# Three transposes per 128 slots in place of two, and a different order at the start of a conv-and-experts kernel

## The chip, the cores and the metric

The kernel runs on one core of one Trainium2 chip. The metric is the device time of that core in microseconds (us), less is better. Times of the kernel before are the median of three runs; a profiled execution stands beside them.

## What is computed

Two stages, in float32, over 8 sequences of 3584 tokens with 192 channels each. The first is a causal convolution along the sequence, with 7 taps per head (8 heads of 24 channels), the taps normalised by a softmax. The second sends each token through one of 8 experts:

```python
logits = x @ w_gate                       # 8 per token
local  = sigmoid(x @ w_local)
for each token s of a sequence, in order:
    fresh = argmax(logits[s])
    e = fresh if s == 0 or local[s] < 0.5 else prev_e
    prev_e = e
    h = maximum(x[s] @ w1[e], 0)          # 192 -> 1024
    out[s] = softmax(logits[s])[e] * (h @ w2[e])   # 1024 -> 192
```

A token may thus take the expert of the token before it, so the choice is a scan along the sequence.

## The kernel before

**Parts, slots and blocks.** The 28672 tokens are cut into 16 parts of 1792 (`PT`). A part is convolved, its experts are chosen (routing), and each of its rows, with its weight, number and channels, is scattered to a slot of its expert in DRAM (`slots`, one indirect DMA per 128 or 112 rows, issued by POOL in `put`, L777). A block is one or two units of 128 slots of one expert. The first 35 blocks have one unit each, then come 87 blocks of two units and 20 of one (142 in all, 229 units of 128 slots). Which expert a block belongs to is worked out on the chip (`first_table`, `table`) and read by SP from `tabi` when it loads the block's rows (L913) and weights (L906). A block may load its rows once the scatters of its group of parts are done. Four buffers hold weights, six hold rows.

**A block.** `hidden` multiplies the rows, turned so that channels lie on partitions, with the first weights (L963); ScalarE applies the relu and writes `hT` (L968). `turn` then transposes the rows of the next block on TensorE (L360) and ScalarE copies the result out of PSUM to `xT`. `output` multiplies `hT` with the second weights into two PSUM tiles `yps` (L980), one per half of the contraction; ScalarE scales one (L988), VectorE adds the other (L992), and POOL sends the rows to `out` (L996). There are two `yps` buffers in all, so a block's two tiles are those that the block before used. TensorE works on two halves of 64 rows at a time, and a row of 192 channels is three groups of 64 (`KD`, `DR`). A row in DRAM holds its 192 channels and a repeat of 64 of them.

In `turn`, the kernel before transposes channels 0 to 127 and then channels 128 to 191 with their repeat. Each half of the rows goes to all 128 partitions, so the second transpose gives the third group on both halves of the partitions, and the three groups are brought into place by three ScalarE copies: L947 on 128 partitions, and L949 twice on 64.

**The convolution.** The first two parts are convolved on TensorE (`wide`), the others on VectorE: ScalarE writes the first tap of a head (L378), VectorE adds the six others (L388), 48 such operations per part. `conv` is a generator; `step(time)` takes operations from it, or from a part's routing, until their estimated times add up to `time`. `step` stands between the pieces of a block. The order in which instructions are written is the order in which each engine runs them.

**The start.** `wide_route` is the routing of the first two parts in pieces that end at a `yield`: (1) and (2) the best logit, the exponent and `fc`; (3) the transposes to `rps` on TensorE; (4) the scan to `run`, its transpose `bps`, and the norm; (5) `oh` and its sums on TensorE; (6) slots (`upto`, `pos`), after which 16 scatters are ready to be put; (7) the tables. The first two blocks don't read their rows from DRAM: VectorE builds 0/1 matrices (`hots`, L550), TensorE gathers the rows with them (`gather`, L556), and ScalarE copies them out (`gathered`, L561 to L563). The kernel before interleaves the gathers with the whole of `route1`, the second part's routing, and issues the 16 scatters of the first part in groups of 5, 3, 2, 2 and 4, all but the first group each after a named instruction of `route1` (`puts_behind`). Then the blocks begin.

Of the kernel before, what the change touches and what calls it, by code (L numbers as in the profile page):

```python
# [17 lines left out]
P = 128  # L18
# [63 lines left out]
def kernel(  # L82
# [100 lines left out]
        nc.vector.tensor_copy(c.rearrange("p h k -> p (h k)"), cps[:, H:H + H * KC])  # L183
    wgb, wgq = wg[:, :3, :], wg[:, 3:, :]

    got, mark = {}, {}

# [7 lines left out]
    def wide(g, xv, y_sb, both):  # L195

        lps = yps_p.tile([P, 512], F32, name="yps")[:, :4 * TB].rearrange("p (q s) -> p q s", s=TB)  # L200
        count = [0]

        def mine():
            count[0] += 1
            return both and count[0] % 2 == 0

        def convolve(half, heads):
            bs = slice(half * NH, (half + 1) * NH)
            for h in heads:
                ps = hps_p.tile([P, 512], F32, name="hps")[:TB, :NH * GS]  # L210
                nc.tensor.matmul(ps, lhsT=hank[:NI, h, :],
                                 rhs=xv[:NI, bs, h * GS:(h + 1) * GS], start=True, stop=True)
                to = y_sb[:TB, bs, Y0 + h * GS:Y0 + (h + 1) * GS]
                at = ps.rearrange("p (b d) -> p b d", d=GS)
                if mine():
                    nc.vector.tensor_scalar(to, at, rz[:TB, h:h + 1], None, Alu.mult)
                else:
                    nc.scalar.activation(to, at, Act.Copy, scale=rz[:TB, h:h + 1])
                yield

        def again(half):
            bs = slice(half * NH, (half + 1) * NH)
            nc.gpsimd.tensor_copy(yr[:, bs, :], y_sb[:TB, bs, Y0 + P:Y0 + D])
            nc.gpsimd.tensor_copy(y_sb[:TB, bs, Y0 + D:IX], y_sb[:TB, bs, Y0 + P:Y0 + D])

        def turned(half, qs):
            at = half * 3 * NH // 2
            for q in qs:
                tps = hps_p.tile([P, 512], F32, name="hps")[:, :4 * TB].rearrange(
                    "p (u s) -> p u s", s=TB)  # L230
                for u in range(4):
                    b = half * NH + (q * 4 + u if q < 2 else 2 * u)
                    src = (y_sb[:TB, b, Y0:Y0 + P] if q < 2
                           else yr[:, b:b + 2, :].rearrange("p b d -> p (b d)"))
                    nc.tensor.transpose(tps[:, u, :], src, identity=ident[:TB, :TB])
                leave = nc.vector.tensor_copy if mine() else nc.scalar.copy
# [26 lines left out]
        products()  # L263
        if both:
            nc.vector.tensor_copy(lsb[:, :2, :], lps[:, :2, :])
            nc.scalar.copy(lsb[:, 2:, :], lps[:, 2:, :])
        else:
            nc.scalar.copy(lsb, lps)
        yield
        ltp = yps_p.tile([P, 512], F32, name="yps")[:TB].rearrange("p (q c) -> p q c", c=P)  # L270
        for q in range(4):
            nc.tensor.transpose(ltp[:, q, :], lsb[:, q, :], identity=ident)
        lt = sm.tile([P, NB, E + 1], F32, name="lt")[:TB]
        mark["lt", g] = nc.vector.tensor_copy(lt.rearrange("p (j q) e -> p j q e", q=4),
                              ltp.rearrange("p q (j c) -> p j q c", c=Q)[:, :, :, :E + 1])
        got[g] = lt

# [116 lines left out]
    def wide_route(g, y_sb, lt):  # L394
# [41 lines left out]
        yield  # L436
        run = sm.tile([NB, TB], F32, name="run")
        nf = sm.tile([NB, TB], F32, name="nf")
        mark["nf", g] = nc.vector.tensor_copy(nf, rps[:, 1, :])
# [20 lines left out]
        if g:  # L460
            norm()
        yield
        oh = sm.tile([P, E, NB], F32, name="oh", bufs=1)[:TB]
        mark["oh", g] = nc.vector.tensor_tensor(oh, bcast_mid(bps, E), bcast(en[:TB], NB),
                                                op=Alu.is_equal)


# [8 lines left out]
        mark["upto", g] = nc.vector.tensor_tensor_scan(upto.rearrange("p e b -> p (e b)"),  # L476
                                     go_on.rearrange("p e b -> p (e b)"),
                                     nps[:, :E * (1 + NB)], 0.0, Alu.mult, Alu.add)
        at = sm.tile([P, E, NB], F32, name="at", bufs=1)[:TB]
# [23 lines left out]
    def first_table(upto, pos):  # L503
# [24 lines left out]
        nc.vector.scalar_tensor_tensor(rel, bcast(r2[:TB], NB), -float(UT), bcast_mid(pos, 2),  # L528
                                       Alu.mult, Alu.add)
        rels.append(rel)  # L530
        hots(0)

        inn = sm.tile([P, E], F32, name="inn")
        nc.vector.tensor_scalar(inn, end[:, :E], i_of, None, Alu.is_le)
# [24 lines left out]
    def gathered(ps):  # L559
        xg = xp.tile([P, KT, DG], F32, name="xg")  # L560
        nc.scalar.copy(xg[:, 0, :Y0 + D], ps[:, :Y0 + D])  # L561
        nc.scalar.copy(xg[:, 0, Y0 + D:IX], ps[:, Y0 + P:Y0 + D])
        nc.scalar.copy(xg.bitcast(I32)[:, 0, IX:], ps[:, 1:2])  # L563
        return xg

    def logits(g, y_sb):

        nc.gpsimd.tensor_copy(y_sb[:, :, Y0 + D:IX], y_sb[:, :, Y0 + P:Y0 + D])  # L568
# [361 lines left out]
    def turn(n, xg):  # L930


        xps = xps_p.tile([P, 2, 512], F32, name="xps")
        at = xps[:, :, :BT].rearrange("p h (d k s) -> p h d k s", d=2, k=KT)
        for d in range(2):
            for k in range(n):
                src = xg[:, k, Y0 + d * P:Y0 + (d + 1) * P]
                for half in range(2):
                    turn_half(at[:, half, d, k, :], src, half)
        xT = tp.tile([P, KD, BT], F32, name="xT")  # L940
        to = xT.rearrange("p d (k h s) -> p h d k s", k=KT, h=2)
        first, by = to[:, :, :2], at
        if n == KT:
            first, by = [a.rearrange("p h d k s -> p h (d k) s") for a in (first, by)]
        else:
            first, by, to, at = [a[:, :, :, 0, :] for a in (first, by, to, at)]
        nc.scalar.copy(first, by)  # L947
        for half, rows in halves():
            copied = nc.scalar.copy(to[rows, :, 2], at[(DR, 0)[half]:(P, DR)[half], :, 0])  # L949
        return xT, copied  # L950

    def hidden(n, wb, xT, shares=(1, 1)):
# [124 lines left out]
    for n in (4, 3, 5, 1, 3, 0):  # L1077
        next(route0)
        some(wide1, n)

    def puts_behind(ins, n):
        for _ in range(n):
            put(ins)

    puts_behind(None, 5)
    rest(route0)
    some(wide1, WIDE - 20)

# [23 lines left out]
    weights(AHEAD - 1)  # L1112


    picks = [yps_p.tile([P, 512], F32, name="yps")]
    gather(0, ya, picks[0], range(4))
    rest(wide1)
    puts_behind(mark["lt", 1], 3)
    route1 = wide_route(1, yb, got.pop(1))
    some(route1, 2)  # L1120
    hots(1)
    gather(0, ya, picks[0], range(4, NB))
    next(route1)
    xgs[0] = gathered(picks[0])
    picks.append(yps_p.tile([P, 512], F32, name="yps"))
    gather(1, ya, picks[1], range(9))
    next(route1)
    puts_behind(mark["nf", 1], 2)
    step(1.8)
    xT, _ = turn(blocks[0][1], xgs[0])  # L1130
    gather(1, ya, picks[1], range(9, NB))
    next(route1)
    puts_behind(mark["oh", 1], 2)
    step(2.4)
    xgs[1] = gathered(picks[1])
    next(route1)
    puts_behind(mark["upto", 1], 4)
    rest(route1)
    for i, (_, n, _, _) in enumerate(blocks):
        st["block"] = i  # L1140
        ensure(i)
        weights(i + AHEAD)
        if i == LATE:
            x_in[3] = load_x(3)
        hT = hidden(n, wbs[i], xT, (1, 1) if i else (0, 0))
        if i + 1 < len(blocks):
            xT, copied = turn(blocks[i + 1][1], xgs[i + 1])
            if len(to_put) > NT // 2 and n == KT:
                put(copied)
        step(2.1 if n == 1 else 4.2)  # L1150
        output(n, wbs.pop(i), xgs.pop(i), hT)
        step(1.3 if n == 1 else 3.0)

    kind, _, at, group = spare[0]
# [13 lines left out]
def _w1_layout(np, w1):  # L1168


    w = w1.reshape(E, KD, DR, 2, F // 2).transpose(0, 3, 2, 1, 4)
    w = np.stack([w[:, 0][:, :, [0, 2, 1]], w[:, 1][:, :, [1, 2, 0]]], 1)
    return w.reshape(E, P, KD * F // 2)


# [57 lines left out]
```

## Time and profile before

| What | Value |
|---|---|
| Median of three runs | 1340.45 us (1338.32 to 1340.85) |
| The profiled execution, its time | 1340.85 us |
| The profiled execution, its span | 1339.1 us |
| Mean granted TensorE clock | 0.994 |
| Start of the first block's `hidden` | 50.96 us |
| Period of a block of 256 slots, in the middle | 10.68 us |
| Period of a block of 128 slots, at the end | 5.45 us |

The span begins with the first instruction that the profiler recorded; times below are counted from there. Busy shares overlap, since engines work side by side. "PE" is TensorE's products, "PEld" its weight loads, "DVE" VectorE, "ACT" ScalarE. A group `L980 PE MATMUL yps<-wb,hT` is all instructions of line 980 that write `yps` from `wb` and `hT`; float32 products appear as two instructions each, transposes as one. In a timeline a row is a run of like instructions: start, length of the run, engine, line, operands, count, and, in brackets, the idle time of the engine just before it with what ended it.

### The profile page before, as it was taken

The page shows a single profiled execution, that of the slowest core. Times are in us where ns is not written, and L with a number is a line of the kernel's source. Part 1 is how long each engine was busy: PE and PEld are TensorE (multiplying, and loading weights), DVE is VectorE, ACT ScalarE, POOL GpSimd, SP SyncE. Part 2 cuts the span into 40 slices and gives each one's busy share as a digit, 9 for nine tenths or more (in the row PEclk, how much of TensorE's full clock was granted, in tenths as well). Part 3 has the DMA queues.
Part 4 walks back from the last instruction along what each step waited for, and adds up shares of the span by engine and source line. Part 5 has one row for each costly group of instructions (what it writes and reads, how often), then busy time and mean ns, then how long its engine had stood idle before and what let it go on. Part 6 is the DMA issues. An engine that isn't in the chain of part 4 may idle for free. (4 is left out here: it accounts for less than half of the span.)

```text
span 1339.1 us, 41274 instructions
## 1 busy us (share of the span) xinstructions
PE 1315.2 (98%) x16682; PEld 1264.3 (94%) x16682; DVE 778.6 (58%) x2434; ACT 583.9 (44%) x1431; POOL 492.8 (37%) x538
## 2 busy tenths in 40 slices
PE   8899999999999999999999999999999999999997
PEld 7898999899999999999999999999999999999997
DVE  5878887877777777868786878786520000000000
ACT  5244544444444444444444444444334333334443
POOL 4455443534343434343434343434344211121111
PEclk9899999999999999999999999999999999999999
DMA  4799999977575857675767675756566655556893
GB/s 180 262 357 406 376 352 356 365 281 276 192 287 189 295 197 286 209 274 208 274 209 274 208 281 207 288 204 234 206 234 230 207 185 184 190 192 235 322 332 124
DMA packets 67298, 340.36 MB, mean 254 GB/s; under 512 B 12576, under 2 KB 23191, under 8 KB 47650
## 3 DMA queue, kind: packets, MB, share of 16 engines
q1 hardware_dynamic: 44784, 284.88, 59.2%
q0 software_dynamic: 22320, 52.82, 10.4%
q8 instruction: 133, 2.18, 0.6%
q14 instruction: 59, 0.48, 0.1%
q10 hardware_dynamic: 2, 0.00, 0.0%
HBM read 284.73 MB, written 53.41 MB: 253 GB/s over the span
## 5 line engine op out<-in xcount | busy, mean ns | idle before, releaser
L980 PE MATMUL yps<-wb,hT 64*128 64x192 f32 x7328 | 647.0, 326 | 8.2 <-ACT hT L968 5.3
L963 PE MATMUL hps<-xT,wb 64*128 64x256 f32 (+1 forms) x6816 | 634.5, 336 | 1.6 <-issue 1.2
L980 PEld LDWEIGHTS yps<-wb,hT 64*128 64x128 f32 x7328 | 603.7, 187 | 19.6 <-ACT hT L968 10.8
L963 PEld LDWEIGHTS hps<-xT,wb 64*128 64x128 f32 x6816 | 585.1, 187 | 28.7 <-issue 3.2
L996 POOL DMA_INDIRECT out_dram<-o_sb,xg x229 | 232.4, 1015 | 608.6 <-DVE o_sb L992 540.1
L968 ACT ACTIVATE hT<-hps 128x512 f32<-128x512 f32 (+1 forms) x568 | 262.1, 512 | 393.1 <-PE hps L963 271.6
L388 DVE SCALAR_TENSOR_TENSOR y_sb<-x_sb,c,y_sb 128x336 f32<-128x336 f32 x672 | 376.1, 569 | 20.1 <-ACT y_sb L378 2.0
L992 DVE SCALAR_TENSOR_TENSOR o_sb<-yps,xg,o_sb 128x192 f32<-128x192 f32 x229 | 87.5, 413 | 475.7 <-ACT o_sb L988 468.5
L777 POOL DMA_INDIRECT slots<-y_sb,posi x228 | 228.0, 1000 | 207.4 <-ACT hT L968 81.6
L988 ACT ACTIVATE o_sb<-yps,xg 128x192 f32<-128x192 f32 x229 | 86.9, 418 | 305.4 <-PE yps L980 299.7
L949 ACT COPY xT<-xps 64x256 f32<-64x256 f32 (+1 forms) x284 | 92.4, 325 | 7.0
L947 ACT COPY xT<-xps 128x512 f32<-128x512 f32 (+1 forms) x142 | 72.2, 509 | 5.9 <-PE xps L360 2.9
L360 PEld LDWEIGHTS xps<-ident,xg 64*128 64x128 f32 x916 | 60.2, 139 | 5.2
L378 ACT ACTIVATE y_sb<-x_sb,c 128x336 f32<-128x336 f32 x112 | 63.7, 581 | 1.0
L360 PE MATMUL xps<-ident,xg 64*128 64x64 f32 x916 | 60.3, 221 | 0.0
L572 DVE STREAM_TRANSPOSE z<-y_sb 128x768 f32<-128x768 f32 (+1 forms) x56 | 45.4, 852 | 0.4
L598 DVE COPY lt<-lq 32x36 f32<-32x36 f32 x224 | 41.0, 183 | 3.5
L582 PE MATMUL hps<-z,wg 64*32 64x128 f32 x1344 | 24.1, 272 | 0.7 <-issue 0.5
L582 PEld LDWEIGHTS hps<-z,wg 64*32 64x32 f32 x1344 | 19.0, 105 | 3.1 <-issue 2.3
L556 PE MATMUL yps<-y_sb 112*128 112x194 f32 x64 | 13.8, 377 | 1.8 <-DVE y_sb L550 1.8
L556 PEld LDWEIGHTS yps<-y_sb 112*128 112x128 f32 x64 | 12.5, 220 | 2.6 <-DVE y_sb L550 2.0
L568 POOL COPY y_sb<-y_sb 128x896 f32<-128x896 f32 x14 | 13.4, 954 | 0.0
(240 smaller groups left out, 384.0 us busy)
## 6 DMA issues: line engine op xcount, KB each, us to landing
wb<-in_w_dram SPq DMA_DIRECT2D x138, 1536.0 KB
x_sb<-in_x_dram SPq DMA_DIRECT2D x14, 1920.0 KB
xg<-slots SPq DMA_DIRECT2D x87, 259.0 KB
xg<-slots SPq DMA_DIRECT2D x53, 129.5 KB
wb<-in_w_dram SPq DMA_DIRECT2D x12, 512.0 KB
out_dram<-o_sb,xg POOLq DMA_INDIRECT x229
slots<-y_sb,posi POOLq DMA_INDIRECT x228
x_sb<-in_xb_dram SPq DMA_DIRECT2D x4, 768.0 KB
```

Of the source, the lines that this page charges most:

```text
L360: nc.tensor.transpose(to, src[rows], identity=ident[rows, rows])
L378: nc.scalar.activation(cols(h), chans(h, 0), Act.Copy, scale=c[:, h, 0:1])
L388: nc.vector.scalar_tensor_tensor(cols(h), chans(h, k), c[:, h, k:k + 1], cols(h), Alu.mult, Alu.add)
L777: ins = nc.gpsimd.indirect_dma_start(out=slots[:, :], in_=rows, in_offset=None, out_offset=bass.IndirectOffsetOnAxis(ap=to, axis=0)).ins
L947: nc.scalar.copy(first, by)
L949: copied = nc.scalar.copy(to[rows, :, 2], at[(DR, 0)[half]:(P, DR)[half], :, 0])
L963: nc.tensor.matmul(hps[half][:, j, w], lhsT=wb[rows, f0:f0 + P], rhs=xT[rows, d, w], start=(d == 0 and j == 0), stop=(d == KD - 1), skip_g ...
L968: relu = nc.scalar.activation(hT[:, m:m + 2, w], hps[half][:, :, w], Act.Relu)
L980: nc.tensor.matmul(yps[half][:, k * D:(k + 1) * D], lhsT=hT[rows, m, k * P:(k + 1) * P], rhs=wb[rows, WA + m * D:WA + (m + 1) * D], start= ...
L988: nc.scalar.activation(o_sb[:, k, :], y[k][0], Act.Copy, scale=xg[:, k, 0:1])
L992: nc.vector.scalar_tensor_tensor(o_sb[:, k, :], y[k][1], xg[:, k, 0:1], o_sb[:, k, :], Alu.mult, Alu.add)
L996: sent = nc.gpsimd.indirect_dma_start(out=out, in_=o_sb[:, k, :], in_offset=None, out_offset=bass.IndirectOffsetOnAxis(ap=xg.bitcast(I32)[ ...
```

## The change

- `turn` makes three transposes per 128 slots and half in place of two: channels 0 to 127, 64 to 191, and 128 to 191 with a repeat of channels 0 to 63. The repeat in each row is accordingly the first 64 channels in place of the last 64 (three copies have another source). All three groups then lie in place on all partitions, and one ScalarE copy takes the place of three. The order of the first weights on the host is changed to match.
- The 16 scatters of the first part are issued in one row, as soon as their slots are known, with no instruction to wait behind.
- Both `hots`, both gathers, the turn of block 0 and both `gathered` come first, with nothing of `route1` between them; then nine operations of the convolution (`step(5.4)`), the end of `wide1`, and pieces 1 and 2 of `route1`. Pieces 3, 4 and 5 are put into blocks 0 and 1, pieces 6 and 7 ahead of block 2.
- The second part's scatters, now known later, are put from block 2 on, three in each of blocks 2 and 3.

```diff
@@ first_table
         rels.append(rel)
-        hots(0)
@@ gathered (and likewise in wide's again and in logits)
-        nc.scalar.copy(xg[:, 0, Y0 + D:IX], ps[:, Y0 + P:Y0 + D])
+        nc.scalar.copy(xg[:, 0, Y0 + D:IX], ps[:, Y0:Y0 + DR])
@@ turn
-        at = xps[:, :, :BT].rearrange("p h (d k s) -> p h d k s", d=2, k=KT)
-        for d in range(2):
+        at = xps[:, :, :KD * BT // 2].rearrange("p h (d k s) -> p h d k s", d=KD, k=KT)
+        for d in range(KD):
             for k in range(n):
-                src = xg[:, k, Y0 + d * P:Y0 + (d + 1) * P]
+                src = xg[:, k, Y0 + d * DR:Y0 + (d + 2) * DR]
                 for half in range(2):
                     turn_half(at[:, half, d, k, :], src, half)
...
-        first, by = to[:, :, :2], at
         if n == KT:
-            first, by = [a.rearrange("p h d k s -> p h (d k) s") for a in (first, by)]
+            to, at = [a.rearrange("p h d k s -> p h (d k) s") for a in (to, at)]
         else:
-            first, by, to, at = [a[:, :, :, 0, :] for a in (first, by, to, at)]
-        nc.scalar.copy(first, by)
-        for half, rows in halves():
-            copied = nc.scalar.copy(to[rows, :, 2], at[(DR, 0)[half]:(P, DR)[half], :, 0])
+            to, at = [a[:, :, :, 0, :] for a in (to, at)]
+        copied = nc.scalar.copy(to, at)
@@ the start
-    puts_behind(None, 5)
+    while to_put:
+        put()
     rest(route0)
     some(wide1, WIDE - 20)
...
-    picks = [yps_p.tile([P, 512], F32, name="yps")]
-    gather(0, ya, picks[0], range(4))
+    for i in range(2):
+        hots(i)
+        pick = yps_p.tile([P, 512], F32, name="yps")
+        gather(i, ya, pick, range(NB // 2))
+        if i:
+            xT, _ = turn(blocks[0][1], xgs[0])
+        gather(i, ya, pick, range(NB // 2, NB))
+        xgs[i] = gathered(pick)
+    step(5.4)
     rest(wide1)
-    puts_behind(mark["lt", 1], 3)
     route1 = wide_route(1, yb, got.pop(1))
     some(route1, 2)
-    hots(1)
-    gather(0, ya, picks[0], range(4, NB))
-    next(route1)
-    xgs[0] = gathered(picks[0])
-    picks.append(yps_p.tile([P, 512], F32, name="yps"))
-    gather(1, ya, picks[1], range(9))
-    next(route1)
-    puts_behind(mark["nf", 1], 2)
-    step(1.8)
-    xT, _ = turn(blocks[0][1], xgs[0])
-    gather(1, ya, picks[1], range(9, NB))
-    next(route1)
-    puts_behind(mark["oh", 1], 2)
-    step(2.4)
-    xgs[1] = gathered(picks[1])
-    next(route1)
-    puts_behind(mark["upto", 1], 4)
-    rest(route1)
@@ the loop over blocks
-        hT = hidden(n, wbs[i], xT, (1, 1) if i else (0, 0))
+        if i == 2:
+            rest(route1)
+        hT = hidden(n, wbs[i], xT, {0: (0, 0), 2: (1, 2), 3: (1, 2)}.get(i, (1, 1)))
         if i + 1 < len(blocks):
             xT, copied = turn(blocks[i + 1][1], xgs[i + 1])
             if len(to_put) > NT // 2 and n == KT:
                 put(copied)
+        if i < 2:
+            next(route1)
         step(2.1 if n == 1 else 4.2)
         output(n, wbs.pop(i), xgs.pop(i), hT)
+        if i == 1:
+            next(route1)
         step(1.3 if n == 1 else 3.0)
```

More of the change, by code (lines that the diff above doesn't have):

```diff
@@ L184 @@
     wgb, wgq = wg[:, :3, :], wg[:, 3:, :]
-    got, mark = {}, {}
+    got = {}
     def z_tile():
@@ L223, in again @@
             nc.gpsimd.tensor_copy(yr[:, bs, :], y_sb[:TB, bs, Y0 + P:Y0 + D])
-            nc.gpsimd.tensor_copy(y_sb[:TB, bs, Y0 + D:IX], y_sb[:TB, bs, Y0 + P:Y0 + D])
+            nc.gpsimd.tensor_copy(y_sb[:TB, bs, Y0 + D:IX], y_sb[:TB, bs, Y0:Y0 + DR])
         def turned(half, qs):
@@ L273, in wide @@
         lt = sm.tile([P, NB, E + 1], F32, name="lt")[:TB]
-        mark["lt", g] = nc.vector.tensor_copy(lt.rearrange("p (j q) e -> p j q e", q=4),
+        nc.vector.tensor_copy(lt.rearrange("p (j q) e -> p j q e", q=4),
                               ltp.rearrange("p q (j c) -> p j q c", c=Q)[:, :, :, :E + 1])
@@ L438, in wide_route @@
         nf = sm.tile([NB, TB], F32, name="nf")
-        mark["nf", g] = nc.vector.tensor_copy(nf, rps[:, 1, :])
+        nc.vector.tensor_copy(nf, rps[:, 1, :])
         nc.vector.tensor_tensor_scan(run, nf, rps[:, 0, :], 0.0, Alu.mult, Alu.add)
@@ L463, in wide_route @@
         oh = sm.tile([P, E, NB], F32, name="oh", bufs=1)[:TB]
-        mark["oh", g] = nc.vector.tensor_tensor(oh, bcast_mid(bps, E), bcast(en[:TB], NB),
+        nc.vector.tensor_tensor(oh, bcast_mid(bps, E), bcast(en[:TB], NB),
                                                 op=Alu.is_equal)
@@ L475, in wide_route @@
         upto = sm.tile([P, E, 1 + NB], F32, name="upto")
-        mark["upto", g] = nc.vector.tensor_tensor_scan(upto.rearrange("p e b -> p (e b)"),
+        nc.vector.tensor_tensor_scan(upto.rearrange("p e b -> p (e b)"),
                                      go_on.rearrange("p e b -> p (e b)"),
@@ L566, in logits @@
     def logits(g, y_sb):
-        nc.gpsimd.tensor_copy(y_sb[:, :, Y0 + D:IX], y_sb[:, :, Y0 + P:Y0 + D])
+        nc.gpsimd.tensor_copy(y_sb[:, :, Y0 + D:IX], y_sb[:, :, Y0:Y0 + DR])
         z = z_tile()[:, :NT * D].rearrange("p (t d) -> p t d", d=D)
@@ L1079 @@
         some(wide1, n)
-    def puts_behind(ins, n):
-        for _ in range(n):
-            put(ins)
-    puts_behind(None, 5)
+    while to_put:
+        put()
     rest(route0)
@@ L1171, in _w1_layout @@
     w = w1.reshape(E, KD, DR, 2, F // 2).transpose(0, 3, 2, 1, 4)
-    w = np.stack([w[:, 0][:, :, [0, 2, 1]], w[:, 1][:, :, [1, 2, 0]]], 1)
+    w = np.stack([w[:, 0], w[:, 1][:, :, [1, 2, 0]]], 1)
     return w.reshape(E, P, KD * F // 2)
```

## The prediction

> **What bounds the kernel now.** I read the page's busy shares first, then the timeline of TensorE at two blocks (one of 256 slots, one of 128), then the timelines of VectorE and ScalarE from 31 to 80 us, where the moved work lies.
>
> ```profile
> PE 1315.2 (98%) x16682; PEld 1264.3 (94%) x16682; DVE 778.6 (58%) x2434; ACT 583.9 (44%) x1431; POOL 492.8 (37%) x538
> L360 PE MATMUL xps<-ident,xg 64*128 64x64 f32 x916 | 60.3, 221 | 0.0
> ```
>
> TensorE is busy for 98% of the span, so an instruction added to its stream in a block lengthens the run, unless it falls into a wait. The second line is the transposes: 916 = 229 groups of 128 slots x 4. Its 60.3 us overlap with neighbours, so the price is read from starts:
>
> ```profile
> 504.19 5.48 PE L963 MATMUL hps<-xT,wb 64*128 64x256 f32 x48
> 509.37 0.42 PE L360 MATMUL xps<-ident,xg 64*128 64x64 f32 x6
> 509.61 0.38 PE L980 MATMUL yps<-wb,hT 64*128 64x192 f32 x1
> 514.87 5.48 PE L963 MATMUL hps<-xT,wb 64*128 64x256 f32 x48
> ...
> 1324.16 0.29 PE L360 MATMUL xps<-ident,xg 64*128 64x64 f32 x4
> 1324.28 2.83 PE L980 MATMUL yps<-wb,hT 64*128 64x192 f32 x32
> ```
>
> A 256-slot block takes 514.87 - 504.19 = 10.68 us. From its first transpose to the first product of `output` are 509.61 - 509.37 = 0.24 us for four pairs (one transpose per half of the rows), 0.060 us a pair. In the 128-slot block it is 1324.28 - 1324.16 = 0.12 us for two pairs, again 0.060.
>
> The start is different. VectorE's timeline:
>
> ```profile
> 38.28 2.48 DVE L550 TENSOR_TENSOR y_sb<-rel,wb 112x512 f32<-112x512 f32 x4
> 42.03 0.26 DVE L439 COPY nf<-hps 16x112 f32<-16x112 f32 x1 [1.26 <-PE yps L556]
> ...
> 44.93 2.31 DVE L388 SCALAR_TENSOR_TENSOR y_sb<-x_sb,c,y_sb 128x336 f32<-128x336 f32 x4
> ...
> 60.31 3.47 DVE L388 SCALAR_TENSOR_TENSOR y_sb<-x_sb,c,y_sb 128x336 f32<-128x336 f32 x6
> 63.69 0.41 DVE L992 SCALAR_TENSOR_TENSOR o_sb<-yps,xg,o_sb 128x192 f32<-128x192 f32 x1
> ```
>
> Between 31.9 and 75 us VectorE has only two gaps over half a microsecond, 1.26 and 0.72 us (before L476 at 51.06). So it, not TensorE, sets the pace there. It reaches TensorE through `yps`: `output` of a block can't write its second half before L992 of the block before has read it. L992 ends at 63.69 + 0.41 = 64.10; TensorE issues one product of block 1's `output` at 63.79 and the rest after that. ScalarE's timeline shows what feeds the convolution on VectorE:
>
> ```profile
> 41.98 0.32 ACT L561 COPY xg<-yps 128x194 f32<-128x194 f32 x1 [3.86 <-PE yps L556]
> ...
> 42.35 1.07 ACT L378 ACTIVATE y_sb<-x_sb,c 128x336 f32<-128x336 f32 x2
> ```
>
> L388 can't start before L378, and L378 stands on ScalarE behind whatever was issued before it.
>
> **What the Trainium skill says.** "TensorE: Matmul & The Clock Gate", section "LDWEIGHTS (loading the stationary operand)", prices a load by its columns, 128 / 1.2 = 107 ns. In the trace, transposes that share a half of the rows follow each other at about 60 ns with a load of 128 columns each; the measurement decides, and 107 ns stays as an upper estimate. The same page, Part 1, says that TensorE falls to half clock after a mostly idle window of about 3.4 us. The trace agrees: after the idle stretch from 42.3 to 44.3 us, the window 45 to 51 us has a granted clock of 0.50. "PSUM — Partial Sum Buffer", section "Engine vs sequencer instructions", calls the queues of ScalarE and VectorE strict FIFO; the L378 above, just behind the L56x copies, agrees.
>
> **The change, part by part.**
>
> *Transposes.* Three pairs in place of two per 128 slots: one more pair, two transposes with their two weight loads. 229 x 0.060 = +13.7 us. Where TensorE waits for `hT` behind the turn, the extra pair is hidden: the waits list 18 such waits (L980 for L968), 18 x 0.060 = 1.1 us. From below 12.6; above, by the page's load price, 229 x 0.107 = 24.5, and by L360's busy time, 60.3 / 458 = 0.132 a pair, 30.1 us. I take **+13**.
>
> *ScalarE's copies.* One copy in place of three per block. Before: 592 + 2 x 367 ns (256 slots), 377 + 2 x 260 ns (128 slots). The slope from 377 to 592 ns over 256 elements puts the new copy at 0.81 and 0.49 us. That frees 87 x 0.52 + 55 x 0.41 = 68 us of ScalarE. Its path value is nothing: `xT` is wanted only after `output`, 2.6 or 5.1 us later, and TensorE's waits for `xT` sum to 0.9 us in the run. The changed sources at L224, L562 and L568 and the weight order on the host cost nothing: same sizes, same engine.
>
> *Scatters in one row.* POOL issues one each 1.25 us from 30.43; sixteen begin by 49.2 in place of 55.5. The row load of block 2, which waits for all of them on SP (issued at 58.51, 3.0 us after the last scatter began), and the weights of block 3 behind it (60.31) move some 6 us ahead. `tabi` is written 2.6 us earlier because `hots(0)` moves behind it, so SP's first nine weight loads begin near 34.0 instead of 36.5. Four more scatters fall into their transfer; nothing waits behind them on POOL, whose next job is at 64.4. Neither load is what VectorE waits for, so I count no gain from them.
>
> *Routing spread over blocks.* Durations from VectorE's timeline: rest of the first table 1.5 us, each `hots` 2.5, `lt` and the first two steps of `route1` 2.4, step four 3.0 (1.95 to `run`), step five 0.95, steps six and seven 9.3, one L388 0.58. In the new order:
> - VectorE: table to 33.4, `hots(0)` to 36.0, `hots(1)` to 38.5. TensorE gathers from 34.2: 32 instructions at 0.165 us to 39.5, half of the second gather to 42.1, turn, the other half to 45.0.
> - The second `gathered` now stands ahead of the first L378 on ScalarE (before, L378 ran at 42.35). 0.65 + 0.6 us: the first L388 starts near 46.3. VectorE is idle for 7.8 us.
> - Nine L388 to 51.5, then `lt` and two steps to 53.9. TensorE has run block 0's `hidden` (45.5 to 48.4) and stands at the `rps` transposes, which wait for that `fc`: 5.3 us idle, with `output(0)` behind them.
> - Six L388 to 57.4, L992(0), three L388, step four to 62.5. `bps` on TensorE waits for `run` until 61.7, ahead of `output(1)`.
> - Six L388, L992(1) and `oh` to 66.7. TensorE waits 1.6 us for `oh` and starts `hidden(2)` near 67.6 (before: 66.5).
> - 2.4 us more, then the 9.3 us of steps six and seven, six L388, L992(2): done near 82.3. `output(3)` would be ready at 76.1 and waits for it. `hidden(4)` starts near 85.0; before, it started at 78.50: +6.5.
>
> Before, the same L992(2) ended at 75.1, and `output(3)` started near 75.85: VectorE had 0.7 us to spare, later 1.2. So the 7.8 us of idle time, less the 2 us of gaps that go, reach TensorE nearly whole. Idle stretches of 5.3 and 6.2 us bring half-clock windows of 3.4 us, 1.7 us each; the first is covered by VectorE, the second not wholly. From block 5 to 9 a little comes back where blocks ran at 5.8 to 6.9 us beside full DMA queues. I take **+7**. Below: VectorE does not bind, `hidden(0)` starts at 45.2 and five blocks run at 5.5 to 72.8 instead of 84.58, -11.8. Above: while scatters are issued, TensorE's completions reach others late (the first gather's products had run by 34.55 + 4.11 = 38.7, ScalarE began L561 at 41.98); two such handovers at 3 us on top, +13.
>
> **Sum.** 13 + 7 = +20. The profiled execution took 1340.85 us for a span of 1339.1; that run is 0.4 above the median. So the span goes to 1359 and the median from 1340.45 to **1360.5**.
>
> **Rivals.**
> - *The start is a wash.* The lost idle time is made up because L378 is issued earlier than I read, or by the earlier loads. For it: the order of loads does improve by 6 us. Against: VectorE had no spare time. 13 + 0: 1353.
> - *Not slower.* One mechanism: the start is bound by TensorE and the loads, not by VectorE. Then block 5 starts 11.8 us earlier, against +12.6 for the transposes: 1341. It needs VectorE to lose less than 1 us between 38 and 75; against it is L992(0), at whose end TensorE resumes.
> - *Dearer.* Either the loads set the transposes' price (+24.5 to +30) or late completions meet the whole row of scatters (+13 at the start): 1367 to 1378.
> - *The turn is not what the diff says*, the third pair being hidden throughout: only the start counts, 1347. Against it: no wait lies in a 10.68 us block.
>
> **How the numbers follow.** Main case 70%, own range 1356 to 1366; the wash 14%; dearer 10%; not slower 4%; turn hidden 2%. About 0.2%, 2.7 us, is what a measurement of this kernel can tell from no change. The main case, the wash and the dearer one are slower beyond it. The not-slower case is half within 0.2%, half beyond it on the fast side. Slower 0.96, same 0.02, faster 0.02. The range 1351 to 1368 holds the main case, the wash and the near end of the dearer one.
>
> **What would show it.** L360 x1374; 0.36 us from the first transpose to `output` in a 256-slot block, whose period goes to 10.80; tail blocks from 5.45 to 5.51. One L949-like copy per block of 128x768 or 128x384. On VectorE a gap of 7 to 9 us before the first L388, which starts after 45; `hidden(0)` near 45.5 and `hidden(4)` after 84. If the gap is there but `hidden(4)` starts before 80, VectorE was not the bound and the start's step fails. If the period stays 10.68, the transposes' step fails.

## The result, and the profile after

The changed kernel takes 1388.07 us (four runs, 1382.50 to 1389.54) beside 1339.84 for the kernel before: **slower by 48.2 us**, a ratio of 1.0353 (95% interval 1.0323 to 1.0384). Forecast were 1360.5 and a range up to 1368. The profiled execution took 1389.54 us for a span of 1387.7, at a mean clock of 0.987. Line numbers of the changed kernel differ a little: its L549, L555, L560, L581, L586, L959, L964, L976, L984, L988 and L992 are L550, L556, L561, L582, L587, L963, L968, L980, L988, L992 and L996 of the kernel before.

The page of the changed kernel, its busy shares and the group of the transposes:

```profile
PE 1341.1 (97%) x17140; PEld 1291.4 (93%) x17140; DVE 784.1 (57%) x2434; ACT 511.0 (37%) x1147; POOL 489.1 (35%) x538
...
L360 PE MATMUL xps<-ident,xg 64*128 64x64 f32 x1374 | 77.2, 222 | 9.7 <-ACT xg L560 9.7
```

TensorE is busy 26 us longer, at a share of 97% in place of 98%: the rest of the 48 us is new idle time. TensorE's timeline at two blocks in the middle and two at the end (start, length, instruction, operands, count):

```profile
1000.36 5.35 PE L959 MATMUL hps<-xT,wb 64*128 64x256 f32 x48
1005.54 0.54 PE L360 MATMUL xps<-ident,xg 64*128 64x64 f32 x12
1005.91 5.43 PE L976 MATMUL yps<-wb,hT 64*128 64x192 f32 x64
1011.16 5.35 PE L959 MATMUL hps<-xT,wb 64*128 64x256 f32 x48
...
1364.46 2.85 PE L959 MATMUL hps<-xT,wb 64*128 64x128 f32 x48
1367.14 0.35 PE L360 MATMUL xps<-ident,xg 64*128 64x64 f32 x6
1367.32 2.83 PE L976 MATMUL yps<-wb,hT 64*128 64x192 f32 x32
1369.97 2.85 PE L959 MATMUL hps<-xT,wb 64*128 64x128 f32 x48
```

The periods are 1011.16 - 1000.36 = 10.80 and 1369.97 - 1364.46 = 5.51, both as predicted. The transposes are not where the forecast failed. TensorE's timeline at the start, in brackets the idle time before a row and what ended it:

```profile
31.14 9.84 PE L555 MATMUL yps<-y_sb 112*128 112x194 f32 x48 [2.92 <-DVE y_sb L549]
50.64 0.58 PE L360 MATMUL xps<-ident,xg 64*128 64x64 f32 x6 [9.67 <-ACT xg L560]
...
56.74 2.95 PE L959 MATMUL hps<-xT,wb 64*128 64x128 f32 x48
...
65.62 0.53 PE L426 MATMUL hps<-ident,fc 112*16 112x112 f32 x2 [5.75 <-ACT hT L964]
...
95.05 5.17 PE L976 MATMUL yps<-wb,hT 64*128 64x192 f32 x29 [3.64 <-DVE o_sb L988]
99.69 0.63 PE L959 MATMUL hps<-xT,wb 64*128 64x128 f32 x2
```

The first gather (32 of the 48 products in the first row) and half of the second are done at 41; then TensorE waits 9.67 us for the copy L560 of the first gather's rows. `hidden(0)` starts at 56.74, not near 45.5, and `hidden(4)` at 99.69, 21.2 us after the 78.50 of the kernel before. The first gather's copy and the first taps on ScalarE, and the row additions on VectorE:

```profile
50.27 0.32 ACT L560 COPY xg<-yps 128x194 f32<-128x194 f32 x1 [20.77 <-remote]
...
56.78 1.54 ACT L378 ACTIVATE y_sb<-x_sb,c 128x336 f32<-128x336 f32 x3
```
```profile
57.43 5.89 DVE L388 SCALAR_TENSOR_TENSOR y_sb<-x_sb,c,y_sb 128x336 f32<-128x336 f32 x10 [22.05 <-ACT y_sb L378]
```

VectorE's gap is 22.05 us in place of the 7.8 forecast, and L560 waits for "remote": the semaphore that it waits for was raised when no instruction that raises it had just ended. The products it reads were done; the report of their end came later. The blocks after that show a further loss. The lag behind the kernel before is 23.3 us at block 34 and 45.2 at block 104; 70 blocks of two units at 0.12 make 8.4 of these 22. The rest falls on pairs of blocks around each part's logits (L581), whose groups on the page changed; below them the same copy in the kernel before:

```profile
L581 PE MATMUL hps<-z,wg 64*32 64x128 f32 x1344 | 30.7, 273 | 5.3 <-issue 5.0
...
L586 ACT COPY ls<-hps 128x128 f32<-128x128 f32 x28 | 6.1, 269 | 40.3 <-remote 27.4
...
L587 ACT COPY ls<-hps 128x128 f32<-128x128 f32 x28 | 6.1, 269 | 10.1 <-PE hps L582 10.1
```

ScalarE is idle for 40.3 us ahead of this copy in place of 10.1, and TensorE itself for 5.3 us between the products of the logits.

### The profile page after: what moved, and what is told of

Its sections match the earlier page's. It is cut to its first block, busy times and chain, and to the rows that moved or that the text cites. A ratio compares the mean times of both kernels' runs of the same rounds, so it can differ in the third digit from the quotient of the medians.

```text
span 1387.7 us, 41896 instructions
## 1 busy us (share of the span) xinstructions
PE 1341.1 (97%) x17140; PEld 1291.4 (93%) x17140; DVE 784.1 (57%) x2434; ACT 511.0 (37%) x1147; POOL 489.1 (35%) x538
## 3 DMA queue, kind: packets, MB, share of 16 engines
q0 software_dynamic: 22320, 52.82, 10.1%
## 5 line engine op out<-in xcount | busy, mean ns | idle before, releaser
L976 PE MATMUL yps<-wb,hT 64*128 64x192 f32 x7328 | 649.6, 327 | 9.4 <-ACT hT L964 5.3
L959 PE MATMUL hps<-xT,wb 64*128 64x256 f32 (+1 forms) x6816 | 641.0, 337 | 2.6 <-issue 1.4
L976 PEld LDWEIGHTS yps<-wb,hT 64*128 64x128 f32 x7328 | 608.5, 188 | 17.7 <-ACT hT L964 11.7
L959 PEld LDWEIGHTS hps<-xT,wb 64*128 64x128 f32 x6816 | 594.8, 188 | 26.7 <-issue 8.0
L992 POOL DMA_INDIRECT out_dram<-o_sb,xg x229 | 231.7, 1012 | 638.0 <-DVE o_sb L988 565.4
L388 DVE SCALAR_TENSOR_TENSOR y_sb<-x_sb,c,y_sb 128x336 f32<-128x336 f32 x672 | 383.1, 582 | 71.6 <-issue 30.2
L964 ACT ACTIVATE hT<-hps 128x512 f32<-128x512 f32 (+1 forms) x568 | 261.9, 512 | 397.9 <-PE hps L959 300.2
L988 DVE SCALAR_TENSOR_TENSOR o_sb<-yps,xg,o_sb 128x192 f32<-128x192 f32 x229 | 87.1, 412 | 442.8 <-ACT o_sb L984 424.7
L984 ACT ACTIVATE o_sb<-yps,xg 128x192 f32<-128x192 f32 x229 | 86.8, 418 | 386.7 <-PE yps L976 365.3
L945 ACT COPY xT<-xps 128x768 f32<-128x768 f32 (+1 forms) x142 | 97.0, 683 | 2.5 <-PE xps L360 1.2
L360 PEld LDWEIGHTS xps<-ident,xg 64*128 64x128 f32 x1374 | 77.7, 139 | 13.8 <-ACT xg L560 10.0
L360 PE MATMUL xps<-ident,xg 64*128 64x64 f32 x1374 | 77.2, 222 | 9.7 <-ACT xg L560 9.7
L581 PE MATMUL hps<-z,wg 64*32 64x128 f32 x1344 | 30.7, 273 | 5.3 <-issue 5.0
L581 PEld LDWEIGHTS hps<-z,wg 64*32 64x32 f32 x1344 | 21.1, 105 | 13.6 <-issue 10.9
L589 DVE STREAM_TRANSPOSE lq<-ls 128x256 f32<-128x256 f32 x14 | 6.2, 444 | 41.8 <-ACT ls L586 41.8
L586 ACT COPY ls<-hps 128x128 f32<-128x128 f32 x28 | 6.1, 269 | 40.3 <-remote 27.4
L555 PE MATMUL yps<-y_sb 112*128 112x194 f32 x64 | 15.1, 410 | 2.9 <-DVE y_sb L549 2.9
L555 PEld LDWEIGHTS yps<-y_sb 112*128 112x128 f32 x64 | 14.5, 248 | 3.5 <-DVE y_sb L549 3.3
```

What stands on the lines that cost most here:

```text
L360: nc.tensor.transpose(to, src[rows], identity=ident[rows, rows])
L388: nc.vector.scalar_tensor_tensor(cols(h), chans(h, k), c[:, h, k:k + 1], cols(h), Alu.mult, Alu.add)
L581: nc.tensor.matmul(lps[half][Q * j:Q * j + Q, :], lhsT=wgq[rows, b, :], rhs=z[rows, begin[j]:begin[j] + TQ, b * Q:(b + 1) * Q], start=(b = ...
L945: copied = nc.scalar.copy(to, at)
L959: nc.tensor.matmul(hps[half][:, j, w], lhsT=wb[rows, f0:f0 + P], rhs=xT[rows, d, w], start=(d == 0 and j == 0), stop=(d == KD - 1), skip_g ...
L964: relu = nc.scalar.activation(hT[:, m:m + 2, w], hps[half][:, :, w], Act.Relu)
```

## Theories

- **Late reports.** While scatters are under way, other engines hear late that TensorE has finished. A row of sixteen is one long stretch without reports; and the logits now stand where the output scatters are.
- **Order alone.** The chain of waits in the new order is longer than worked out, without any delay of reports.
- **Loads.** The nine weight loads in the same stretch delay the copies, not the scatters.
- **Shift of the logits.** `step(5.4)` takes ten row additions ahead of the blocks, where the kernel before takes eight; all later parts are then ready one `step` earlier, and their logits land between `output` and the next `hidden` in place of between `turn` and `output`.

Each run in the table stands beside runs of the kernel before on the same chip. The chips differed: the kernel before took 1338 to 1340 us on some and 1320 on others, and this turned out to be the key. after_again, after_there and after_fourth are the changed kernel once more.

| Run | us | Kernel before, us | Ratio (95%) |
|---|---|---|---|
| turn_only | 1332.59 | 1320.20 | 1.0088 (1.0071 to 1.0105) |
| start_only | 1329.54 | 1320.20 | 1.0060 (1.0043 to 1.0077) |
| row_only | 1319.77 | 1320.20 | 0.9994 (0.9985 to 1.0003) |
| held_back | 1330.28 | 1320.20 | 1.0081 (1.0058 to 1.0104) |
| after_again | 1388.06 | 1337.75 | 1.0380 (1.0363 to 1.0398) |
| held_after | 1380.63 | 1337.75 | 1.0318 (1.0301 to 1.0335) |
| eight_ops | 1374.50 | 1337.75 | 1.0278 (1.0261 to 1.0295) |
| row_again | 1351.41 | 1337.75 | 1.0104 (1.0087 to 1.0121) |
| after_there | 1385.35 | 1338.22 | 1.0346 (1.0324 to 1.0368) |
| start_eight | 1361.65 | 1338.22 | 1.0181 (1.0164 to 1.0198) |
| late_puts | 1354.33 | 1338.22 | 1.0115 (1.0099 to 1.0132) |
| after_late_puts | 1389.85 | 1338.22 | 1.0384 (1.0366 to 1.0401) |
| after_fourth | 1346.30 | 1320.61 | 1.0199 (1.0183 to 1.0214) |
| late_puts_some | 1320.25 | 1320.61 | 1.0000 (0.9991 to 1.0009) |

## The experiments

**The two halves of the change, one by one.** turn_only is the kernel before with the new `turn` (and its order of rows and weights); start_only is the changed kernel with the old one.

> The kernel before with the two-transpose turn (and the layout of rows and weights that goes with it), its start left as it was. All theories of the start agree here: 229 more pairs of transposes at 0.060 us, 13 us, so 1353 (1351 to 1356, ratio 1.009 to 1.012); blocks of two tiles 0.12 us longer, the tail's 0.06, and hidden(0) and the fifth block where they were before. If the turn also costs time at the start or unsettles the parts' logits, the total lies above 1358 and the excess is seen before the first two-tile block or in the parts.

> The changed kernel with the three-transpose turn put back: the new order of the start alone. If the transposes are worth 13 us everywhere, this stands 13 below the changed kernel: 1375 (1372 to 1378, ratio 1.024 to 1.028). hidden(0) at 56 to 57 and the fifth block near 99 as in the changed kernel, and the parts' logits again one step early (12 us of the 35). As the prediction had the start, it would be 1347.

The turn cost 12.4 us, as expected. The start cost 9.3, not 35. The kernel before took 1320 here, so either the halves hurt each other or this chip doesn't show what the first one did. A miss for the expectation of 1375, which took the first chip's delays as a property of the kernel.

**The row of scatters by itself.** In the kernel before:

```diff
-    puts_behind(None, 5)
+    puts_behind(None, 16)
...
-    puts_behind(mark["upto", 1], 4)
```

> The kernel before with all 16 scatters of the first part in one row and nothing else moved (the later places find none to put). If a row of scatters holds back the report of TensorE's products until it has drained, the copies of the first gather wait until the row's end near 50 us, and hidden(0) goes from 51 to 56 or later: 1346 to 1360 in all. If the order of the routing is the cause and the row is innocent, hidden(0) stays within 1 us of 51 and the total at 1340 (1337 to 1343).

> The kernel before with its 16 scatters in one row, a second time. On a chip where the kernel before takes 1320 again: the same as it (ratio 0.998 to 1.001). On a chip where it takes 1340: if a row of scatters delays TensorE's reports there, hidden(0) at 56 or later and 1346 to 1360; if the row is innocent there too, 1337 to 1343.

On the chip where the kernel before takes 1320 the row costs nothing. On the one where it takes 1338 it costs 13.7 us. The same kernel, twice; ScalarE's timeline of row_only, then of row_again:

```profile
35.76 0.32 ACT L561 COPY xg<-yps 128x194 f32<-128x194 f32 x1 [0.58 <-PE yps L556]
```
```profile
50.65 0.32 ACT L561 COPY xg<-yps 128x194 f32<-128x194 f32 x1 [15.21 <-remote]
```

The first gather's products on TensorE in row_only:

```profile
31.61 4.11 PE L556 MATMUL yps<-y_sb 112*128 112x194 f32 x24
```

TensorE's and VectorE's timelines of row_again, and the last of the sixteen scatters on POOL's:

```profile
31.85 4.11 PE L556 MATMUL yps<-y_sb 112*128 112x194 f32 x24
35.80 0.35 PE L426 MATMUL hps<-ident,fc 112*16 112x112 f32 x2
```
```profile
50.69 0.26 DVE L439 COPY nf<-hps 16x112 f32<-16x112 f32 x1 [12.62 <-remote]
```
```profile
46.73 0.94 POOL L777 DMA_INDIRECT slots<-y_sb,posi  x1 [0.30 <-issue]
```

Both runs have the same products at nearly the same time: the first gather ends at 31.61 + 4.11 = 35.72 in row_only and at 31.85 + 4.11 = 35.96 in row_again. On one chip ScalarE starts its copy at once. On the other, ScalarE (50.65) and VectorE (50.69, for L426's result) both hear of it 14.7 us later, within 0.04 us of each other and 3 us after the end of the last scatter's issue at 47.67. Two engines that wait for different products and go on together: the delay is in TensorE's report, not in ScalarE. The traces confirm it, since they also record when a semaphore was raised. In row_again TensorE's raises for the products that ended at 35.96, 36.15, 39.28 and 40.37 stand at 50.63, 50.67, 50.83 and 50.87; in row_only each of these four stands within 0.02 us of the end of its product. I call chips with this behaviour late, the others prompt.

All sixteen traces fall into these two kinds. Of the some 1000 recorded raises of TensorE's semaphore, 143 to 253 lie more than 0.1 us from the end of every TensorE instruction that raises it in each of the ten traces on late chips, and 26 to 29 in each of the six on prompt ones. VectorE, ScalarE and POOL have 3 to 5 such raises each in every trace. In before, after and row_again the middle half of TensorE's displaced raises comes 0.38 to 0.65 us after POOL has ended the issue of a scatter.

**The scatters moved, the loads left.** In the start alone (held_back) and in the changed kernel (held_after), 4 scatters go free and 12 wait for the last copy of the second block's rows (`last` holds the last copy of each `gathered`; the lines of later code are two further down):

```diff
-    while to_put:
-        put()
+    for _ in range(4):
+        put()
...
         xgs[i] = gathered(pick)
+    while to_put:
+        put(last[1])
     step(5.4)
```

> The start alone (three transposes), with 4 scatters free and the other 12 behind the last copy of the second block's rows: only the scatters' place differs from the run of the start alone. If the row holds back TensorE's report, the first gather's copies run as soon as its products end, hidden(0) comes at 46 to 49 in place of 56 to 57, and the total falls by 5 to 10 us to 1365 to 1370, less whatever the later row (some 15 us from about 46) does to blocks 0 and 1. If the weight loads or ScalarE's own queue hold the copies, hidden(0) stays at 56 and the total at 1375 or above, since the rows of block 2 then land later.

> The changed kernel with 4 scatters free and the other 12 behind the last copy of the second block's rows. Where reports of TensorE are prompt, the row costs nothing and this stays within 3 us of the changed kernel. Where they are late and the row is what delays them, the first gather's copies run 8 to 12 us earlier, hidden(0) comes before 50 instead of at 56.7, and the total lies 5 to 10 us below the changed kernel. If late reports come from weight loads or from the chip alone, hidden(0) stays near 56.

held_back met a prompt chip: 1330.28 beside 1329.54, no difference, which tells nothing of the theories. held_after met a late one. Its timelines of ScalarE, POOL and SP's queue:

```profile
38.53 0.32 ACT L562 COPY xg<-yps 128x194 f32<-128x194 f32 x1 [8.16 <-PE yps L555]
...
61.49 0.38 ACT L966 ACTIVATE hT<-hps 128x256 f32<-128x256 f32 x1 [7.67 <-issue]
```
```profile
31.67 0.98 POOL L778 DMA_INDIRECT slots<-y_sb,posi  x1 [0.30 <-issue]
45.10 0.94 POOL L778 DMA_INDIRECT slots<-y_sb,posi  x1 [12.45 <-ACT xg L564]
...
58.84 0.94 POOL L778 DMA_INDIRECT slots<-y_sb,posi  x1 [0.30 <-issue]
```
```profile
31.25 7.17 SPq L907 DMA_DIRECT2D wb<-in_w_dram  x9
```

With no scatter issued between 32.65 and 45.10 the copy runs at 38.53, as soon as its gather is done, while the nine weight loads are issued in that very stretch: loads alone don't delay the report. `hidden(0)` starts at 44.66 in place of 57.17. But the delay moves with the row: it now hits block 0, whose `hidden` ends at 47.61 and whose last two relus wait until 61.49 and 62.23; the first of them starts 1.7 us after the last scatter's issue. Of the 12.5 us, 6.8 are left at block 4, and 7.4 in the total. The 5 to 10 us that were expected came.

**Ten row additions or eight.** `step` subtracts 0.6 until nothing is left; taking 0.6 nine times from 5.4 leaves a tiny rounding error, so a tenth operation is taken. With

```diff
-    step(5.4)
+    step(4.5)
```

the changed kernel takes eight.

> The changed kernel with 8 row additions of the fourth part ahead of the first block in place of 10, the number of the kernel before. If the number sets in which half of a block all later parts' logits land, they return to their place between turn and output (the block after the one of the changed kernel), and where reports are late the total falls by 9 to 14 us, where they are prompt by less than 2. If the parts' extra time comes from late reports wherever the logits stand, nothing falls on either chip.

The logits went back to their place (one part's L581 at 366.06, between the transposes and `output`), and the total fell by 1388.06 - 1374.50 = 13.6 us. Waits of after_again, then of eight_ops (engine, line, releaser, us in total, times, longest):

```profile
ACT ls L586 <- remote: 31.5, 10, 3.6
...
ACT ls L586 <- PE hps L581: 8.2, 5, 3.5
```
```profile
ACT ls L586 <- PE hps L581: 17.1, 14, 2.3
```

The "remote" waits of this copy are gone. One part's logits in after_again (TensorE, ScalarE and POOL):

```profile
364.63 1.59 PE L581 MATMUL hps<-z,wg 64*32 64x128 f32 x96
...
369.18 3.02 PE L959 MATMUL hps<-xT,wb 64*128 64x256 f32 x24 [0.17 <-ACT ls L586]
```
```profile
368.86 0.43 ACT L586 COPY ls<-hps 128x128 f32<-128x128 f32 x2 [3.57 <-remote]
```
```profile
365.99 0.99 POOL L992 DMA_INDIRECT out_dram<-o_sb,xg  x1 [3.40 <-DVE o_sb L988]
367.28 0.99 POOL L992 DMA_INDIRECT out_dram<-o_sb,xg  x1 [0.30 <-issue]
```

and in after_fourth, on a prompt chip:

```profile
333.75 1.70 PE L581 MATMUL hps<-z,wg 64*32 64x128 f32 x96
```
```profile
335.75 0.43 ACT L586 COPY ls<-hps 128x128 f32<-128x128 f32 x2 [1.16 <-PE hps L581]
```
```profile
335.01 0.99 POOL L992 DMA_INDIRECT out_dram<-o_sb,xg  x1 [3.51 <-DVE o_sb L988]
336.30 0.99 POOL L992 DMA_INDIRECT out_dram<-o_sb,xg  x1 [0.30 <-issue]
```

Both have the output scatters of the block before under way when the logits end. On the late chip the copy starts 368.86 - 366.22 = 2.64 us after them, when the second scatter has been issued; on the prompt one 0.30 us after them, in the midst of the scatters. The logits and `hidden` share four `hps` tiles, so the second half of the next `hidden` needs a tile that this copy frees: TensorE starts it at 369.18, behind L586. Between the products of the logits TensorE is idle for 3.4 us in after_again and 0.3 in eight_ops; how the 13.6 us divide between such pauses and such waits was not worked out. On a prompt chip the place of the logits costs next to nothing: in start_only blocks 40 and 41 take 12.30 + 10.79 us, in row_only, with the logits in the old place, 10.68 + 12.44.

**Do the parts add up where reports are late?** start_eight is start_only with `step(4.5)`; after_there is the changed kernel again.

> The start alone (three transposes) with 8 row additions ahead of the first block. If the parts add up where reports are late: 1374.5 less the turn's 13, so 1360 to 1363 (ratio 1.016 to 1.019): the start without the shift of the logits is worth 22 to 25 us there. If the turn costs more than 13 where reports are late, this lies below 1358. Prompt reports: 9 to 10 above the kernel before, since the shift cost nothing there.

> The changed kernel again, beside three others on one chip. If TensorE's reports are late here (the kernel before at about 1338), 1388 and a ratio of 1.036 to 1.039, as twice before. If they are prompt here (the kernel before at about 1320), the two halves' 12.4 and 9.3 us add to 1340 to 1344, a ratio of 1.015 to 1.018: the predicted sum. If it stands above 1350 where the kernel before takes 1320, the halves hurt each other and late reports are not the cause of the missed 28 us.

They do, as far as late chips agree: the changed kernel stood 48.2, 50.3 and 47.1 us above the kernel before in three comparisons there. start_eight stands 23.4 us above the kernel before, and the row alone on a late chip (13.7) with the start where the row costs nothing (9.3) makes 23.0. eight_ops, which has the turn besides, stands 36.75 above it on another late chip: 13.3 for the turn, close to the 12.4 it cost alone. The shift's 13.6 on top makes the 50.3 of after_again.

**Scatters behind the second pair of relus.** In late_puts, the kernel before has

```diff
-        hT = hidden(n, wbs[i], xT, (1, 1) if i else (0, 0))
+        hT = hidden(n, wbs[i], xT, (0, 2) if i else (0, 0))
```

and after_late_puts is eight_ops with (0, 2), and (0, 3) in blocks 2 and 3.

> The kernel before with both of a block's scatters behind the second pair of ReLUs, in place of one behind each pair. Late reports: in blocks 9 to 34 the second pair of ReLUs waited for a report that came with the end of the scatter put ahead of it, 0.59 us a block; with no scatter under way then, those blocks take 5.45 as the others do, and some 25 of them give 10 to 15 us: ratio 0.988 to 0.993. If the delay is not from that scatter but from the block's output scatter or from the weight load, nothing changes (0.998 to 1.002). Prompt reports: nothing to gain (0.998 to 1.002).

> The changed kernel with 8 row additions ahead of the first block and the scatters of a block all behind the second pair of ReLUs. Late reports: 1374.5 of the run with 8 less 10 to 15, so 1360 to 1365 over a kernel before at 1338. If scatters ahead of the second pair don't delay it: 1374 again. Prompt reports: 20 to 24 above the kernel before, as the changed kernel.

Both miss. Beside the profiled kernel before, nine of the twelve blocks near 6.03 us between block 8 and block 35 took 5.45, as expected, but others took longer (block 25 10.31 in place of 8.81), and the stretch took 165.0 us beside 168.3: 3.3 us gained of 10 to 15. From block 35 to the last but one it took 1065.1 beside 1049.1. Two scatters in a row now stand where the parts' logits run (blocks 41 and 47 took 14.4 and 14.5 us in place of 13.1 and 13.0), and there TensorE pauses between its own products, for nothing that the profile shows ("issue"). Its waits at the logits in late_puts, then in the kernel before:

```profile
PE hps L582 <- issue: 9.3, 34, 0.4
```
```profile
PE hps L582 <- issue: 0.5, 2, 0.3
```

after_late_puts took 15 us more than eight_ops on another late chip, with 12.1 us of these pauses in place of 0.3. On prompt chips they are 1.3 us or less. So on a late chip scatters also slow TensorE's own issue; that this has the same cause as the late reports is likely, but not shown. late_puts_some keeps (0, 2) to blocks 7 to 34, and after_fourth is the changed kernel:

> The kernel before with both scatters behind the second pair of ReLUs in blocks 7 to 34 alone. Where reports are late: the run with it everywhere gained 3.3 us over these blocks and lost its 16 in the later blocks and the start, so 3 to 5 below the kernel before (ratio 0.996 to 0.998). If the later blocks' loss came from the rows of these blocks landing later, it stays: 1345 to 1354. Where reports are prompt: 0.999 to 1.001.

> The changed kernel once more, for a chip whose reports are prompt (the kernel before near 1320): there the sum of its halves, 1340 to 1344, ratio 1.015 to 1.018; over 1355 there would say that the halves hurt each other. Where the kernel before takes 1338: 1385 to 1388 again.

Both met a prompt chip. late_puts_some equals the kernel before there; on a late chip it wasn't run, so no version that beats the kernel before is shown. The changed kernel costs 25.7 us there (24.2 to 28.3 by its interval), more than the sum of its halves, 21.7, and 1346.3 in place of the expected 1340 to 1344. At block 35 the start's loss is the same in both traces, 12.4 us in start_only (265.43 - 252.99, beside row_only) and 12.0 in after_fourth (below); why the totals differ by 4 us is open.

## Why the prediction missed

The direction and the transposes were right; the size was not. On a prompt chip the same kernel, at +25.7 us, lies inside the forecast's range of +10.6 to +27.6, though not at its +20; on late chips it stands at +47 to +50. Measured one by one, the terms are 12.4 us for the turn and 9.3 for the order of the start (both on a prompt chip), 13.7 for the row and 13.6 for the shift of the logits (both on a late one): 49.0 in all. The forecast had 13, 7, nothing and nothing.

- **Transposes, +13: right.** 12.4 us alone on a prompt chip, 13.3 by difference on late ones. L360 is x1374, 0.37 us from first transpose to `output` (0.36 forecast), periods 10.80 and 5.51.
- **ScalarE's copies, nothing: right.** One copy per block, 0.81 and 0.49 us; L945 is busy 97.0 us in place of 164.6 for L947 and L949. The 67.6 us freed (68 forecast) bought nothing.
- **"Scatters in one row … I count no gain": the step that failed first.** It looked for who waits behind the scatters on POOL and found nobody. On a late chip the row holds back TensorE's report instead: in the kernel before it cost 13.7 us by itself (row_again), where this step put nothing. The prediction had this mechanism, from the gap between 38.7 and 41.98, but only in the dearer rival and at "two such handovers at 3 us". It was one handover of some 12 us (50.27 in the changed kernel, 38.53 where the row was moved). The stretch without reports grew with the row (14.7 us with sixteen scatters, 2.64 with two), and the rival took it as a fixed price.
- **Start, +7: mis-sized even where reports are prompt.** There its chain can be followed. TensorE's timeline of after_fourth, then VectorE's, then TensorE's of late_puts_some, whose start is that of the kernel before:

```profile
44.88 2.95 PE L959 MATMUL hps<-xT,wb 64*128 64x128 f32 x48
...
53.83 0.53 PE L426 MATMUL hps<-ident,fc 112*16 112x112 f32 x2 [5.81 <-ACT hT L964]
...
72.34 2.65 PE L976 MATMUL yps<-wb,hT 64*128 64x192 f32 x30
...
82.77 5.04 PE L976 MATMUL yps<-wb,hT 64*128 64x192 f32 x29 [4.57 <-DVE o_sb L988]
87.42 0.45 PE L959 MATMUL hps<-xT,wb 64*128 64x128 f32 x2
```
```profile
45.56 5.97 DVE L388 SCALAR_TENSOR_TENSOR y_sb<-x_sb,c,y_sb 128x336 f32<-128x336 f32 x10 [9.81 <-ACT y_sb L378]
```
```profile
44.36 1.82 PE L963 MATMUL hps<-xT,wb 64*128 64x128 f32 x26
...
75.17 0.38 PE L963 MATMUL hps<-xT,wb 64*128 64x128 f32 x2
```

  Forecast against measured: gap on VectorE 7.8 and 9.81 us, first L388 46.3 and 45.56, `hidden(0)` 45.5 and 44.88, TensorE's wait ahead of `output(0)` 5.3 and 5.81, `output(3)` released at 82.3 and 82.77 by L988(2) (L992(2) in the prediction). So the chain through VectorE was read rightly, with 2 us too little for the gap. Two terms were wrong. First, `output(3)` itself: 29 products in 5.04 us after 4.57 us of waiting, where `output(2)` needs 2.65 for 30. The granted clock there is 0.50 (a row shows the stretch, its length, the busy time of each engine, then the clock, the DMA share and GB/s):

```profile
82.70:86.00 3.30, 3.23 (x20) 3.23 (x22) 3.16 (x7) 0.00 (x0) 2.40 (x3) 0.50 0.98 421
```

  The Trainium skill ("TensorE: Matmul & The Clock Gate", Part 1) gives half rate after an idle window of about 3.4 us, and this wait of 4.57 us agrees. The stretch that the prediction cited for it was idle for 2.0 us only, so in that trace less was enough. The prediction priced such a window at 1.7 us, wrote that the second was not wholly covered, and put at most 0.5 us for it (+7 over the +6.5 of its chain); here it costs 2.4. Second, the yardstick: the 78.50 of the kernel before held late reports of its own; on a prompt chip its `hidden(4)` starts at 75.17. The start costs 87.42 - 75.17 = 12.3 us there, of which 12.0 are left at block 35 (268.84 - 254.75, less 35 transpose pairs at 0.06).
- **The shift of the logits: not in the sum at all.** The prediction counted "nine L388"; the page shows x10. It was worth 13.6 us on a late chip and next to nothing on a prompt one.
- **The rivals.** None reached 1388. "Dearer" was the nearest, for its mechanism. "A wash" and "not slower" are out: the start lost 9.3 us by itself even on a prompt chip. "Turn hidden" is out: the period of a block of 256 slots rose to 10.80 us.
- **The theories after the result.** Late reports are shown by the row on two chips, by the scatters moved and by the recorded raises. The order alone costs 9.3 us where reports are prompt. The loads are out, by held_after. The shift of the logits is shown by eight_ops.

What stays open: why some chips report late. The runs tell chips apart by the kernel before (1338 or 1320), but no chip is known to stand in two groups of runs, so they don't show whether it is the chip itself or something that lasted for the time of those runs. Nor was it seen on what path the report and the scatter meet.

## What to carry to other kernels

A wait put down to "remote", or an engine that starts microseconds after the work it waits for has ended, is a cost with a cause: look for what else is under way in that stretch before taking it as a constant. Count who must hear from TensorE while a row of indirect scatters drains, and not only who is queued behind the scatters. Where generators fill time by estimates, a change at the start moves all that follows by a step, so count the operations in the written order, rounding included, and look where the moved work lands.

## What the runs showed of the hardware

- On late chips TensorE's completions don't reach ScalarE or VectorE while indirect scatters follow each other: 14.7 us with sixteen in a row (35.96 to 50.65), 2.64 us with two. On prompt chips, with the same scatters, 0.04 and 0.30 us.
- On late chips TensorE also pauses between its products while scatters are issued: 9.3 us in 34 pauses at the logits of late_puts, 0.5 us in two where the scatters stand elsewhere.
- The other direction wasn't delayed: in after_again VectorE's L549 ran from 31.55, eight in 4.98 us, and TensorE's first gather began at 32.28, one L549 later, with scatters under way; and of the raises of VectorE, ScalarE and POOL only 3 to 5 each are displaced in any trace.
- The kernel before itself probably pays for this: its blocks 10 to 13 take 6.0 us on a late chip and, in row_only, 5.45 on a prompt one, and it takes 1338 against 1320 us in all. That all of the 18 us come from late reports is not shown.
